# Moving transposes from TensorE to the DMA engines in a fused windowed-attention and SwiGLU kernel, with paced loads

## The chip, the cores and the metric

The kernel runs on one core of one Trainium2 chip. The metric is the time of one execution on the device in microseconds (us); lower is better. Each run lists the clock that was granted to TensorE. Executions of one kernel mostly agree within 0.3 to 1%. A single-core execution counts as slow when it is over 1.5% above the fastest of the same kernel; only fast ones are compared here, by the ratios; the medians below are of all runs.

Names: TensorE is PE in the profile (PEld is its weight load), VectorE is DVE, ScalarE is ACT, GpSimd is POOL and SyncE is SP. GpSimd and SyncE also issue the DMA transfers; each engine has one queue of instructions.

## The reference, cut to what matters

```python
# attention: 4 sequences, 8 heads, 768 tokens, 64 wide; 4 sink tokens, window of 128
scores = q @ k.T / sqrt(64)
keep = (key < 4) | ((0 <= query - key) & (query - key < 128))
a = softmax(where(keep, scores, -1e9)) @ v
# then, with x = a as (3072 tokens, 512):
xn = x / rms(x) * rms_g
out = (silu(xn @ w_gate) * (xn @ w_val)) @ w_out      # 512 -> 1536 -> 512
```

The window of 128 means that the keys of one block of 128 tokens are read by the queries of that block and of the next one.

## The kernel before

The 3072 tokens are 24 blocks of 128, six to a sequence. The FFN takes four blocks (a group) at a time. TensorE does FFN matmuls of one group while the attention units of later blocks are woven in between, one block per `step`.

q and k come in with tokens on the partitions, and the score matmuls need them transposed, in the tile `qkT` of a sequence. Blocks 0 to 12 and 18 are transposed by TensorE (eight 128x128 transposes, then copies out of PSUM), the others by DMA transposes from SyncE's queue:

```python
def load_block(src, name, g):
    ...
    tl = ld.tile([P, H, D], BF16, name=name)     # 18 buffers each for q and k
    nc.gpsimd.dma_start(out=tl, in_=...)
...
    load_wo(0)
    last_load = load_wo(1)
with tc.issue_after(last_load):                  # all other loads, as early as GpSimd can
    for g in range(2 * GB, NB):
        load_q(g); load_k(g); load_v(g)          # (three lines in the kernel)

def by_dma(g):
    return g >= DMA_T_FROM and g % NT > 0        # 12 and up, never a sequence's first block

def unit_t(g):
    b, t = divmod(g, NT)
    if by_dma(g):
        for i, src in enumerate((QS.pop(g), KS_.pop(g))):
            nc.sync.dma_start_transpose(
                out=QKT[b][:, i, :, t * P:(t + 1) * P], in_=src.rearrange(...))
        return
    ... # TensorE transposes and a ScalarE copy
```

Three consumers of `qkT` matter. The first is the score unit. Note the width of `rhs`: up to 256 queries, this block's and the next one's.

```python
def unit_s(g):
    b, t = divmod(g, NT)
    nq = 2 if t + 1 < NT else 1
    w = nq * P
    ...
            nc.tensor.matmul(out=..., lhsT=QKT[b][pr, 1, hp, t * P:(t + 1) * P],
                             rhs=QKT[b][pr, 0, hp, t * P:t * P + w], ...)
```

The second is a pair of tiny VectorE copies that gather the four sink keys of a sequence out of its first block:

```python
def unit_sink(b):
    ks = sink.tile([P, HP * KSW], BF16, name="ksk")
    nc.vector.memset(ks, 0.0)
    ...
    for hi in range(2):
        pr = slice(hi * D, (hi + 1) * D)
        nc.vector.tensor_copy(out=ksv[pr, :, hi * NS:(hi + 1) * NS],
                              in_=QKT[b][pr, 1, :, 0:NS])
```

The third is the sink scores, which come later. The normalized x is transposed the same two ways: by TensorE for blocks 0 to 7, by DMA from block 8 (`DMA_X_FROM`).

The order of instructions is fixed by hand only on TensorE and SyncE (`MANUAL`) in the main part. VectorE, ScalarE and GpSimd get their order from the scheduler that builds the program.

The softmax here doesn't subtract the row's maximum and nothing guards it: scores larger than these inputs give would overflow.

## Time and profile before

| | before |
|---|---|
| time, median of 3 | 254.26 us |
| span of the profiled run | 252.6 us |
| TensorE busy | 95% |
| VectorE busy | 72% |
| q and k transposes on TensorE / by DMA (blocks) | 14 / 10 |

From the page of the kernel before: the span, the busy time of each engine, and some rows of the table in 40 slices of 6.3 us (each digit is tenths busy; PEclk is the granted clock in tenths).

```profile
span 252.6 us, 4804 instructions
PE 238.8 (95%) x1733; PEld 127.4 (50%) x1760; DVE 181.1 (72%) x474; ACT 139.6 (55%) x312; POOL 98.1 (39%) x129
...
PE   5988979989999999999999999999999999999994
...
DVE  5666869889779999539989459988359991287700
...
PEclk9999999999999999999999999999999999999999
DMA  9999999999999999650120550321321013200022
```

TensorE is full from about slice 10 (60 us) on, and its clock is never cut. The DMA engines are full for the first 16 slices (to about 101 us; the prediction below says 110), because all loads are issued as early as possible.

The waits of TensorE in the kernel before (what waited, for whom, us in total, times, longest):

```profile
PE pqk L251 <- DMA qs<-in_q_dram: 1.3, 2, 0.7
...
PE pqk L251 <- DMA ks<-in_k_dram: 1.0, 2, 0.6
```

These 2.3 us are TensorE's transposes of blocks 5 and 8 waiting for their loads.

How long a DMA transpose takes from issue to landing depends on what else is on the engines. Two answers of the issue table of the kernel before, one for 70 to 80 us and one for 120 to 140 us (destination, source, queue, operation, count, median us to landing):

```profile
qkT<-qs SPq DMA_TRANSPOSE x1, 8.3
qkT<-ks SPq DMA_TRANSPOSE x1, 8.2
```

```profile
qkT<-qs SPq DMA_TRANSPOSE x1, 2.4
qkT<-ks SPq DMA_TRANSPOSE x1, 2.4
```

Amid the loads it is 8 us, on quiet engines 2.4 us.

### The profile page before, as it was taken

How to read it: one execution, taken by the hardware profiler on the slowest of the kernel's cores; microseconds unless marked ns; L12 is line 12 of the kernel's file. 1: busy time of each engine (PE TensorE's matmuls, PEld its weight loads, DVE VectorE, ACT ScalarE, POOL GpSimd, SP SyncE). 2: the span in 40 equal slices, each digit the busy share in tenths (PEclk: the TensorE clock that was granted, in tenths of full speed). 3: DMA queues.
4: the chain of work that ended last, by engine and by line, in shares of the span. 5: the costliest groups of instructions: out<-in, count | busy, mean ns of one | idle time of the engine just before them, and what ended most of it. 6: DMA issues, size and time to landing. Idle time of an engine off the chain costs nothing.

```text
span 252.6 us, 4804 instructions
## 1 busy us (share of the span) xinstructions
PE 238.8 (95%) x1733; PEld 127.4 (50%) x1760; DVE 181.1 (72%) x474; ACT 139.6 (55%) x312; POOL 98.1 (39%) x129
## 2 busy tenths in 40 slices
PE   5988979989999999999999999999999999999994
PEld 1446858655555454454454454454454544444441
DVE  5666869889779999539989459988359991287700
ACT  2757858879886465556473546466545441323211
POOL 8996779289985763134041004044201000000000
PEclk9999999999999999999999999999999999999999
DMA  9999999999999999650120550321321013200022
GB/s 130 152 174 189 189 156 188 182 155 150 194 186 161 155 131 155 128 168 13 21 56 10 145 145 3 64 58 19 113 84 23 0 21 98 91 0 0 0 86 83
DMA packets 105850, 25.74 MB, mean 102 GB/s; under 512 B 95074, under 2 KB 102754, under 8 KB 105827
## 3 DMA queue, kind: packets, MB, share of 16 engines
q0 software_dynamic: 80704, 13.90, 76.5%
q1 hardware_dynamic: 24082, 11.28, 18.6%
q10 hardware_dynamic: 1040, 0.26, 0.5%
q8 instruction: 14, 0.23, 0.4%
q14 instruction: 10, 0.07, 0.1%
HBM read 28.31 MB, written 6.29 MB: 137 GB/s over the span
## 4 chain that ended last, share of the span: by engine, by line
PE 67%; DMA 12%; DVE 8%; POOL 7%; ACT 2%; issue 2%; POOLq 0%; ACTq 0%; DVEq 0%
PE po L622 23%; PE pvl L581 18%; PE pg L581 18%; DMA wv<-in_moe_w_val_dram 7%; DMA ks<-in_k_dram 5%; PE pT L413 3%; DVE p L599 2%; POOL v L124 2%; POOL qs L111 2%; DVE hT L607 2%; PE pv L456 1%; PE pv L452 1%; PE pv L444 1%; POOL ks L111 1%; ACT et L422 1%
## 5 line engine op out<-in xcount | busy, mean ns | idle before, releaser
L581 PE MATMUL pg<-xnt,wg 128*128 128x512 bf16 (+1 forms) x317 | 73.5, 352 | 1.1 <-ACT xnt L567 0.5
L581 PE MATMUL pvl<-xnt,wv 128*128 128x512 bf16 (+1 forms) x322 | 73.4, 353 | 0.4
L622 PE MATMUL po<-wo,hT 128*128 128x512 bf16 x279 | 64.9, 379 | 0.5 <-issue 0.2
L594 ACT ACTIVATE th<-pg 128x512 bf16<-128x512 f32 x72 | 42.9, 596 | 39.1 <-PE pg L581 39.0
L599 DVE SCALAR_TENSOR_TENSOR p<-th,pg 128x512 bf16<-128x512 bf16 x72 | 48.9, 679 | 20.1 <-ACT th L594 19.5
L607 DVE TENSOR_TENSOR hT<-p,pvl 128x512 bf16<-128x512 bf16 x72 | 49.2, 684 | 3.7 <-PE pg L581 0.5
L581 PEld LDWEIGHTS <-wv 128*128 128x128 bf16 x328 | 30.5, 98 | 27.2 <-issue 1.1
L581 PEld LDWEIGHTS <-wg 128*128 128x128 bf16 x328 | 30.4, 98 | 26.9 <-issue 1.2
L422 ACT ACTIVATE et<-pT 128x512 bf16<-128x512 f32 x76 | 39.8, 602 | 4.8 <-PE pT L413 4.6
L390 POOL TENSOR_SCALAR_AFFINE_SELECT et<-et 128x512 bf16<-128x512 bf16 x20 | 13.1, 660 | 73.9 <-ACT et L422 73.9
L622 PEld LDWEIGHTS <-hT 128*128 128x128 bf16 x288 | 26.7, 98 | 29.7 <-issue 0.8
L494 ACT ACTIVATE sq<-x 128x256 bf16<-128x256 bf16 x48 | 20.0, 417 | 26.5 <-DVE x L484 26.1
L629 ACT ACTIVATE osb<-po 128x512 f32<-128x512 f32 x24 | 14.4, 602 | 25.9 <-PE po L622 20.8
L111 POOL DMA_DIRECT2D qs<-in_q_dram x23 | 20.7, 900 | 7.9 <-DMA wo<-in_moe_w_out_dram 2.2
L124 POOL DMA_DIRECT2D v<-in_v_dram x24 | 21.7, 903 | 4.4 <-DMA qs<-in_q_dram 2.6
L111 POOL DMA_DIRECT2D ks<-in_k_dram x23 | 20.6, 895 | 6.4 <-DMA wo<-in_moe_w_out_dram 3.2
L484 DVE TENSOR_TENSOR x<-pv,rden 128x256 bf16<-128x256 f32 x48 | 20.2, 421 | 0.8
L541 DVE SCALAR_TENSOR_TENSOR xr<-x,y,gb 128x512 bf16<-128x512 bf16 (+1 forms) x25 | 19.8, 795 | 0.7
L479 DVE RECIPROCAL rden<-pv 128x4 f32<-128x4 f32 x48 | 8.4, 175 | 16.1 <-PE pv L456 16.0
L388 DVE TENSOR_TENSOR et<-et,masks 128x1024 bf16<-128x1024 bf16 (+1 forms) x22 | 13.9, 638 | 3.5 <-ACT et L422 3.5
L456 PE MATMUL pv<-v,et 128*128 128x65 bf16 x168 | 15.3, 193 | 0.0
L452 PE MATMUL pv<-v,et 128*128 128x65 bf16 x136 | 12.7, 193 | 0.0
(75 smaller groups left out, 213.1 us busy)
## 6 DMA issues: line engine op xcount, KB each, us to landing
out_dram<-osb SPq DMA_DIRECT2D x24, 256.0 KB, 2.2
v<-in_v_dram POOLq DMA_DIRECT2D x24, 128.0 KB, 7.9
qs<-in_q_dram POOLq DMA_DIRECT2D x23, 128.0 KB, 8.2
ks<-in_k_dram POOLq DMA_DIRECT2D x23, 128.0 KB, 7.7
wg<-in_moe_w_gate_dram POOLq DMA_DIRECT2D x6, 256.0 KB, 7.6
wv<-in_moe_w_val_dram POOLq DMA_DIRECT2D x6, 256.0 KB, 8.2
wo<-in_moe_w_out_dram POOLq DMA_DIRECT2D x2, 768.0 KB, 10.6
osb<-in_k_dram ACTq DMA_DIRECT2D x1, 256.0 KB, 4.8
```

Of the source, the lines that this page charges most:

```text
L111: nc.gpsimd.dma_start(out=tl, in_=src[b, :, t * P:(t + 1) * P, :].rearrange("h t d -> t h d"),)
L124: nc.gpsimd.dma_start(out=V16[b][:, t, :, 0:D], in_=v[b, :, t * P:(t + 1) * P, :].rearrange("h t d -> t h d"),)
L422: nc.scalar.activation(out=et[:, hi].rearrange("p j n c -> p (j n c)"), in_=banks[u][hi], func=ACT.Exp, scale=inv_sqrt_d,)
L456: nc.tensor.matmul(out=dest, lhsT=E[(g, h, 0)], rhs=V16[b][:, t, h, :], start=(t == 0), stop=True, skip_group_check=True,)
L484: nc.vector.tensor_tensor(out=X16[g][:, heads_of(g, u), :], in0=pvv[:, :, 0:D], in1=RDEN.pop((g, u)).unsqueeze(2).to_broadcast((P, 4, D)), ...
L494: nc.scalar.activation(out=sq, in_=xh, func=ACT.Square, scale=MS_SCALE, accum_out=MS[g][:, u:u + 1],)
L541: nc.vector.scalar_tensor_tensor(out=XR[g][-1], in0=x16[:, c], scalar=y[:, 4:5], in1=gb[:, c], op0=ALU.mult, op1=ALU.mult,)
L581: nc.tensor.matmul(out=ps[:, i * n:(i + 1) * n], lhsT=w_sb[:, kt, ft * P:(ft + 1) * P], rhs=XNT[G][:, kt, cols], start=(kt == 0), stop=(kt ...
L594: nc.scalar.activation(out=st["th"], in_=st["pg"], func=ACT.Tanh, scale=0.5)
L599: nc.vector.scalar_tensor_tensor(out=p1, in0=st["th"], scalar=1.0, in1=st["pg"], op0=ALU.add, op1=ALU.mult,)
L607: nc.vector.tensor_tensor(out=HT[key][:, i:i + n, cols], in0=p1.rearrange("p (n c) -> p n c", n=n), in1=pvl.rearrange("p (n c) -> p n c", ...
L622: nc.tensor.matmul(out=st["po"], lhsT=HT[(G, ft // 2)][:, ft % 2, tb * P:(tb + 1) * P], rhs=wo[:, ft, :], start=(ft == 0), stop=(ft == FTN ...
```

## The change

The intent is to relieve TensorE, the fullest engine: transpose q and k from block 5 on, and x from block 4 on, with the DMA engines. The loads are thinned so that the transposes meet less traffic: q and k get four buffers each, so a load waits until the transposes of an earlier block have read their buffer. GpSimd's order is fixed by hand.

```diff
-    DMA_T_FROM = 12
-    DMA_X_FROM = 8
+    DMA_T_FROM = 5
+    DMA_X_FROM = 4
+    LD = 4
+    AHEAD = 6
-    MANUAL = {mybir.EngineType.PE, mybir.EngineType.SP}
+    MANUAL = {mybir.EngineType.PE, mybir.EngineType.SP, mybir.EngineType.Pool}
-    ld = ctx.enter_context(tc.tile_pool(name="ld", bufs=3 * NT))
+    ld = ctx.enter_context(tc.tile_pool(name="ld", bufs=LD))
...
-    with tc.issue_after(last_load):
-        for g in range(2 * GB, NB):
-            load_q(g)
-            load_k(g)
-            load_v(g)
...
     def by_dma(g):
-        return g >= DMA_T_FROM and g % NT > 0
+        return g >= DMA_T_FROM
...  (in step)
-        if g + 2 < NB and not by_dma(g + 2):
-            slots[2 if t != 5 else 1].append(lambda: unit_t(g + 2))
-        if g + 3 < NB and by_dma(g + 3):
+        if g + 3 < NB:
             slots[2].append(lambda: unit_t(g + 3))
+        if g + AHEAD < NB:
+            slots[2].append(lambda: unit_load(g + AHEAD))
...
-        slots = [[lambda: unit_t1(5, 0)], [lambda: unit_t1(5, 1)], [lambda: unit_s(4)], ...
+        slots = [[lambda: unit_t(5)], [lambda: unit_load(8)], [lambda: unit_s(4)], ...
```

The new `by_dma` has lost `g % NT > 0`. The first block of sequences 1, 2 and 3 (blocks 6, 12, 18) is now transposed by DMA too.

More of the change, by code (lines that the diff above doesn't have):

```diff
@@ L238 @@
         load_wo(0)
-        last_load = load_wo(1)
-    with tc.issue_after(last_load):
-        for g in range(2 * GB, NB):
-            load_q(g)
-            load_k(g)
-            load_v(g)
+        load_wo(1)
     QKT, KSK, VSK, ESK, E, X16, MS, XR, XNT = {}, {}, {}, {}, {}, {}, {}, {}, {}
@@ L267, in unit_t1, with unit_load @@
         )
+    def unit_load(g):
+        load_q(g)
+        load_k(g)
+        load_v(g)
     def by_dma(g):
-        return g >= DMA_T_FROM and g % NT > 0
+        return g >= DMA_T_FROM
     def unit_t(g):
@@ L734 @@
         ], first=True)
-        slots = [[lambda: unit_t1(5, 0)], [lambda: unit_t1(5, 1)], [lambda: unit_s(4)], [lambda: unit_sink_scores(0, 4)], [lambda: unit_t(6)], []]
+        slots = [[lambda: unit_t(5)], [lambda: unit_load(8)], [lambda: unit_s(4)], [lambda: unit_sink_scores(0, 4), lambda: unit_load(9)], [lambda: unit_t(6)], [lambda: unit_t(7), lambda: unit_load(10)]]
         for g in range(5, NB + 3):
```

## The prediction

> **What bounds it now.** From about 60 us on, TensorE: the windows view has it 99% busy from 60 to 240 us, and the matmuls started, counted by columns at the pipelined rate that the chain shows (four of 512 columns in 0.86 us), fill 9.5 to 10.1 of each 10 us. At 30–40 and 50–60 us the same count gives 8.0. There the chain of waits runs through loads (the value weights, then k of block 8: 12.5 us from issue to landing), and TensorE's transposes wait for q and k loads, 2.3 us in all (waits view). The page shows the DMA engines at 9 tenths until 110 us: all loads are issued as early as possible. VectorE is close behind: 92% busy at 50–60, 97% at 80–100 us.
>
> **What the change removes.** TensorE transposed q and k for 14 blocks and will for 5: 72 fewer; x for 8 blocks and will for 4: 16 fewer. Four start within 0.22 us in the timeline, so 88 cost 4.9 us. The 2.3 us of waits for loads (blocks 5 and 8) leave TensorE too, and 0.6 us of waits for xr. ScalarE loses about 11 us of copies, worth nothing: it is 55% busy.
>
> **What it adds.** 18 DMA transposes of q/k and 4 of x, each 1.2 us of issue on SyncE's queue, which has room. Landing takes 2.4 us on quiet engines, but 7 to 8 us between 72 and 95 us, where loads saturate them. The Trainium skill ("DMA: Bandwidth & Descriptors", Queues, rings and completion order) says that each DMA engine takes turns between rows by packet, which fits this.
>
> **Critical path.** The weak spot is block 5. Its q and k land at 35.1 and 35.9 us; two issues end near 37.6; landing at 5 to 7.5 us puts the pair at 42.5 to 45. Its scores ran at 42.2 us before; without the transposes and waits ahead of them TensorE would be there at about 39.5. So I expect a new stall of 3 to 5 us there, which eats the early gain. Blocks 6 and 7 should be just in time; block 8 (k landed at 51.6 us, behind wo) may stall up to 1 us. After that the pacing thins the loads, transposes land in 2.4 to 4 us, over a step ahead of use, and the remaining removals (blocks 9–12 and 18, x 4–7) are real. Buffers of four hold up no early load: the transposes that free them precede those issues in the old trace. GpSimd's fixed order should cost nothing. VectorE at 50–100 us may hold back 1 us.
>
> Sum: -4.9 -2.3 -0.6 +3.5 (stalls) +1 (VectorE) = -3.3; stalls may be shorter, so I say -4.
>
> **Predicted: 250.2 us, range 247.0 to 253.3.** Faster by over 2%: 0.36; within 2%: 0.61; slower by over 2%: 0.03.
>
> **What would show it.** 40 q/k transposes left on TensorE of 112, 16 of x of 32; TensorE waiting for a DMA of qkT before block 5's scores, 3 to 5 us in all; DMA digits below 9 from about 50 us but above zero until about 190 us; DMA transposes' median landing under 4 us; ScalarE 11 us less busy.
>
> **What would make it wrong.** Transposes landing in 3 us at 37 us: no stall, near 247. Landing over 8 us, or stalls repeated at blocks 6 to 8: near 254. VectorE the real limit at 50–100 us: no gain there. Masks on GpSimd queued behind loads that wait for buffers: attention late from block 13 on.

## The result, and the profile after

| | before | changed |
|---|---|---|
| time, median of 4 | 254.23 us | 282.31 us |
| ratio, 95% interval | | 1.1105 [1.1058, 1.1153] |
| TensorE busy | 95% | 85% |
| mean granted clock of the profiled run | 1.0 | 0.957 |

A ratio is the mean time of one kernel's fast runs over the mean of the other's fast runs of the same rounds, so it is not quite the ratio of the medians. The changed kernel is correct and 11% slower; the predicted range ended at 253.3 us.

The same lines of the page, for the changed kernel (slices of 7.0 us):

```profile
span 280.1 us, 4727 instructions
PE 239.2 (85%) x1672; PEld 124.1 (44%) x1672; DVE 179.9 (64%) x473; ACT 129.8 (46%) x299; POOL 97.9 (35%) x129
...
PE   6889700099878999999984999999999999999994
...
DVE  5666400569986399973956865798935998067710
...
PEclk9999975579999999999998999999999999999999
DMA  9999999999399999959992999420332100310012
```

The span is longer by 27.5 us and TensorE's busy time is about what it was: the time went into idleness. There is a hole: TensorE shows zeros from 35 to 56 us and VectorE from 35 to 49 us, and in it the clock falls to 5 tenths. Two groups of instructions of the changed kernel's page name it (busy us, mean ns, then idle time of the engine just before them and what ended most of it):

```profile
L298 DVE COPY ksk<-qkT 64x16 bf16<-64x16 bf16 x8 | 1.4, 174 | 31.2 <-DMA qkT<-ks 31.1
L564 PE MATMUL pxt<-ident,xr 128*128 128x128 bf16 x16 | 2.0, 243 | 22.0 <-DVE xr L542 21.9
```

Eight sink-key copies, 1.4 us of work together, have 31.2 us of idle VectorE in front of them. TensorE in turn waits 21.9 us for an xr of VectorE. In the kernel before, the same copies had 0.3 us of idle time before them:

```profile
L297 DVE COPY ksk<-qkT 64x16 bf16<-64x16 bf16 x8 | 1.9, 234 | 0.3 <-ACT qkT L286 0.2
```

VectorE in order of time, 30 to 53 us of the changed kernel (start, duration, instruction, in brackets the idle time before it and who ended it):

```profile
29.81 0.75 DVE L542 SCALAR_TENSOR_TENSOR xr<-x,y,gb 128x512 bf16<-128x512 bf16 x1
...
30.81 0.68 DVE L600 SCALAR_TENSOR_TENSOR p<-th,pg 128x512 bf16<-128x512 bf16 x1
51.99 0.35 DVE L298 COPY ksk<-qkT 64x16 bf16<-64x16 bf16 x2 [20.50 <-DMA qkT<-ks]
52.37 0.16 DVE L504 SCALAR_TENSOR_TENSOR m<-ms 128x1 f32<-128x1 f32 x1
```

Nothing runs on VectorE between 31.5 and 52.0 us. TensorE in the same stretch:

```profile
32.46 1.04 PE L582 MATMUL pvl<-xnt,wv 128*128 128x256 bf16 x8
54.74 0.61 PE L564 MATMUL pxt<-ident,xr 128*128 128x128 bf16 x4 [21.25 <-DVE xr L542]
56.02 1.87 PE L582 MATMUL pg<-xnt,wg 128*128 128x256 bf16 x8 [0.67 <-ACT xnt L568]
```

The queues of the two built programs, which can be listed without running them, show why. VectorE's rows in the kernel before, around the copies of sequence 1:

```
81 L541 TensorScalarPtr xr_720<-x16_677,y_714,gb_97 128x512      (xr of block 3)
82 L264 TensorCopy qkT_284<-pqk_785 128x4x128
...
92 L607 TensorTensor hT_590<-p1_903,pvl_894 128x2x256
93 L297 TensorCopy ksk_1164<-qkT_883 64x4x4 x2                    (sink keys of sequence 1)
```

and in the changed kernel:

```
73 L600 TensorScalarPtr p1_684<-th_657,pg_648 128x512
74 L298 TensorCopy ksk_1073<-qkT_803 64x4x4 x2                    (sink keys of sequence 1)
75 L504 TensorScalarPtr m_632<-ms_601 128x1
...
82 L542 TensorScalarPtr xr_640<-x16_597,y_634,gb_97 128x512      (xr of block 3)
```

In the program text the copies come much later, in step 7. With block 6 no longer transposed by TensorE, whose order is fixed by hand, the scheduler was free to put its reader on VectorE ahead of block 3's xr. On the chip the transpose of block 6's k landed near 52 us, and everything behind the copies waited. The Trainium skill ("TensorE: Matmul & The Clock Gate", specification table) calls VectorE's queue "strict FIFO", which means that it works its instructions off in order; the 20.5 us of idle time agree.

The landings, from the issue table of the changed kernel for 38 to 40.9 us (block 6's q and k):

```profile
qkT<-qs SPq DMA_TRANSPOSE x1, 10.4
qkT<-ks SPq DMA_TRANSPOSE x1, 12.4
```

Over the whole changed kernel the medians are 5.2 us (q) and 4.6 us (k), against 2.4 us before.

The first theory, called Q below, is therefore: the place of the sink-key copies in VectorE's queue costs the time. Rivals: T, the DMA transposes land too late for TensorE itself, and VectorE only shows it; P, the paced loads and GpSimd's order do it. Later names: S, saturated engines make the landings late and the deadline is a block earlier than predicted; P2, the four-deep buffers hold up loads; H, x transposes stand ahead of q and k transposes in SyncE's queue.

### The profile page after: what moved, and what is told of

It reads as the page before. It is cut to its first block, busy times and chain, and to the rows that moved or that the text cites. A ratio compares the mean times of both kernels' runs of the same rounds, so it can differ in the third digit from the quotient of the medians.

```text
span 280.1 us, 4727 instructions
## 1 busy us (share of the span) xinstructions
PE 239.2 (85%) x1672; PEld 124.1 (44%) x1672; DVE 179.9 (64%) x473; ACT 129.8 (46%) x299; POOL 97.9 (35%) x129
## 4 chain that ended last, share of the span: by engine, by line
PE 59%; DMA 19%; DVE 13%; POOL 4%; issue 2%; ACT 1%; SPq 1%; POOLq 0%; DVEq 0%; ACTq 0%
PE po L623 20%; PE pvl L582 17%; PE pg L582 16%; DMA qkT<-ks 8%; DVE hT L608 3%; DMA wv<-in_moe_w_val_dram 3%; DVE p L600 3%; DMA ks<-in_k_dram 3%; DMA qs<-in_q_dram 3%; PE pT L414 2%; DMA qkT<-qs 2%; DVE xr L542 2%; DVE et L389 2%; PE pv L457 1%; PE pv L453 1%
## 5 line engine op out<-in xcount | busy, mean ns | idle before, releaser
L582 PE MATMUL pg<-xnt,wg 128*128 128x512 bf16 (+1 forms) x328 | 75.5, 359 | 2.5 <-ACT xnt L568 1.1
L582 PE MATMUL pvl<-xnt,wv 128*128 128x512 bf16 (+1 forms) x328 | 75.0, 357 | 0.7 <-DVE p L600 0.6
L623 PE MATMUL po<-wo,hT 128*128 128x512 bf16 x288 | 66.1, 379 | 0.8 <-DVE hT L608 0.8
L582 PEld LDWEIGHTS <-wg 128*128 128x128 bf16 x328 | 31.1, 99 | 30.5 <-issue 4.4
L112 POOL DMA_DIRECT2D ks<-in_k_dram x23 | 20.4, 888 | 12.2 <-DMA qkT<-ks 10.7
L298 DVE COPY ksk<-qkT 64x16 bf16<-64x16 bf16 x8 | 1.4, 174 | 31.2 <-DMA qkT<-ks 31.1
L564 PE MATMUL pxt<-ident,xr 128*128 128x128 bf16 x16 | 2.0, 243 | 22.0 <-DVE xr L542 21.9
L414 PE MATMUL pT<-qkT 64*128 64x256 bf16 (+1 forms) x168 | 13.3, 268 | 7.6 <-DVE p L600 4.2
```

The costliest lines, as they stand in the source:

```text
L112: nc.gpsimd.dma_start(out=tl, in_=src[b, :, t * P:(t + 1) * P, :].rearrange("h t d -> t h d"),)
L414: nc.tensor.matmul(out=banks[u][hi][:, j * w:(j + 1) * w], lhsT=QKT[b][pr, 1, hp, t * P:(t + 1) * P], rhs=QKT[b][pr, 0, hp, t * P:t * P + ...
L582: nc.tensor.matmul(out=ps[:, i * n:(i + 1) * n], lhsT=w_sb[:, kt, ft * P:(ft + 1) * P], rhs=XNT[G][:, kt, cols], start=(kt == 0), stop=(kt ...
L623: nc.tensor.matmul(out=st["po"], lhsT=HT[(G, ft // 2)][:, ft % 2, tb * P:(tb + 1) * P], rhs=wo[:, ft, :], start=(ft == 0), stop=(ft == FTN ...
```

## The experiments

| run | what | median us | ratio to before |
|---|---|---|---|
| (changed) | the whole change | 282.31 | 1.1105 |
| e3_ksk_order_only | changed, copies moved back | 268.75 | 1.0528 |
| e6_block6_alone | before, only block 6 by DMA | 273.09 | 1.0696 |
| e13_block6_order | the same, copies moved back | 262.10 | 1.0244 |
| e4_pacing_only | before, with the new loads | 254.82 | 0.9984 |
| e1_first_blocks_on_pe | changed, 6, 12, 18 on TensorE | 265.88 | 1.0434 |
| e7_order_unpaced | e3 with the old loads | 273.10 | 1.0724 |
| e11_wo_later | e3 with wo behind block 8 | 274.09 | 1.0688 |
| e8_from10_x4 | e3, q and k by DMA from block 10 | 259.04 | 1.0154 |
| e9_from10_x8 | e8, x by DMA from block 8 | 254.45 | 1.0001 |
| e10_from10_no_order | e8 without moving the copies | 269.48 | 1.0539 |
| e14_transposes_ahead_of_x | e8, other order on SyncE | 261.93 | 1.0275 |
| e12_from10_8_before_wo | e9, block 8 loaded before wo | 254.67 | 0.9953 |

All gave correct results. The kernel before had medians of 254.68 to 255.53 us beside them; use the ratios between batches. The medians of e9 and e11 hold one slow run each, those of e10 and e12 two; the ratios leave these out.

### e3_ksk_order_only: only the place of the copies

```diff
-            nc.vector.tensor_copy(
-                out=ksv[pr, :, hi * NS:(hi + 1) * NS],
-                in_=QKT[b][pr, 1, :, 0:NS],
-            )
+            with tc.issue_after(LAST_XR[0]) if b > 0 else ExitStack():
+                nc.vector.tensor_copy(...)          # same copy
...  (in unit_xr)
+            LAST_XR[0] = nc.vector.scalar_tensor_tensor(...).ins
```

A listing of the built queues showed VectorE's to differ from the changed kernel's in the place of the copies of sequences 1, 2 and 3 and in nothing else.

> The changed kernel with one thing different: the small VectorE copies that gather the sink keys of sequences 1, 2 and 3 (they read the transposed k of blocks 6, 12, 18) stand later in VectorE's queue, behind the latest xr written before them in the program. Every transfer, buffer and other order is as in the changed kernel. Theory Q (queue order: these copies stand at the head of VectorE's in-order queue long before their DMA transposes land, and hold back everything behind them): the 20.5, 5.3 and 5.4 us idle times of VectorE before these copies go, TensorE's 21.2 us wait for xr goes, and the time falls from 282.3 to 257 us (253 to 262); what stays over 254 is TensorE waiting some 5 to 10 us for DMA transposes of blocks 5, 6 and 8, which landed after 7.6 to 12.4 us. Rival T (late transposes are the cause themselves; VectorE only shows them): TensorE now waits for the same landings at its scores, some 15 to 20 us, and the time stays at 272 us or more. Rival P (the paced loads and GpSimd's order): no change from 282.

Measured: 268.75 us. VectorE no longer waits before the copies, and TensorE's 21 us wait for xr is gone. That is 13.6 us by the medians (about 14.7 by the ratios), from moving six tiny copies. But the time lies between what Q and T expected, because a second wait surfaced. The waits of TensorE in this run:

```profile
PE pT L415 <- DMA qkT<-qs: 14.6, 4, 6.9
```

pT are the scores. In order of time:

```profile
43.92 1.03 PE L415 MATMUL pT<-qkT 64*128 64x256 bf16 x8 [6.86 <-DMA qkT<-qs]
51.01 0.40 PE L415 MATMUL pT<-qkT 64*128 64x128 bf16 x8
56.62 0.61 PE L415 MATMUL pT<-qkT 64*128 64x256 bf16 x8 [0.91 <-DMA qkT<-qs]
65.00 1.04 PE L415 MATMUL pT<-qkT 64*128 64x256 bf16 x8 [4.36 <-DMA qkT<-qs]
...
79.54 0.72 PE L415 MATMUL pT<-qkT 64*128 64x256 bf16 x8 [2.46 <-DMA qkT<-qs]
```

The second line is 128 wide, so it is block 5, the last of its sequence. The line before it is block 4's scores, and they wait for the q of block 5. That is the `rhs` of 256 queries in `unit_s`. In the kernel before, block 4's scores ran at 37.15 us without a wait:

```profile
37.15 0.61 PE L413 MATMUL pT<-qkT 64*128 64x256 bf16 x8
```

The deadline that I had taken, block 5's own scores at 42.18 us, was one block too late. Blocks 6, 7 and 9 wait for the q of 7, 8 and 10 in the same way.

### e6_block6_alone and e13_block6_order: one block, then one block and the order

```diff
 (e6, on the kernel before)
-        return g >= DMA_T_FROM and g % NT > 0
+        return g == 6 or g >= DMA_T_FROM and g % NT > 0
```

> The kernel before with one thing different: block 6 (the first of sequence 1) has its q and k transposed by the DMA engines instead of TensorE, at the same place in the program; all loads are early as before. Theory Q: the scheduler again puts the sink-key copies of sequence 1 ahead of block 3's xr in VectorE's queue (the queue of the built kernel shows it), so VectorE sits idle from about 32 us until the k transpose of block 6 lands, some 7 us after its issue near 39 us; TensorE loses 12 to 15 us, time 266 us (262 to 271), from two transfers out of a kernel's thousands of instructions. Rival T: block 6's scores ran at 47.3 us and the transpose lands at about 46 to 47: no loss, 254 (252 to 256). Rival P: 254.

Measured: 273.09 us, more than Q expected, and far from the 254 of T and P. Two DMA transposes cost 18 us. In the groups of this run the copies show it:

```profile
L297 DVE COPY ksk<-qkT 64x16 bf16<-64x16 bf16 x8 | 1.6, 196 | 17.8 <-DMA qkT<-ks 17.5 <-ACT qkT L286 0.2
```

The k transpose was issued at 39.5 and the copies could start at 50.55 us, a landing of 11.1 us, not the 7 that I used. e13 adds to this the same order fix as in e3.

> The kernel before with only block 6 transposed by the DMA engines (273.1 us with the sink-key copies where the scheduler put them), and those copies moved behind the latest xr before them. Same two DMA transposes, same loads. Theory Q: nearly all of the 18 us goes; TensorE waits for block 6's transpose itself only from block 6's scores on (block 5 is the last of its sequence and does not read block 6), 47.3 us before, and that transpose landed at 50.3: 3 us at most, 256.5 us (254.5 to 258.5). If the copies' place were not the cause, 265 or more.

Measured: 262.10 us, ratio 1.0244 [1.0173, 1.0315], which leaves open whether it is over 2% slower than the kernel before; it is clearly faster than e6 (1.0696). The order is worth 11 of the 18 us; my figure of nearly all was too high. (A few neighbouring VectorE and ScalarE instructions swap places too in the built queues of e13; in e3 none do.) What remains is block 6's own scores waiting for its k, and what that wait does to the clock. TensorE in order of time, then the windows (us, then busy us and count of PE, PEld, DVE, ACT, POOL, then PEclk, DMA share, GB/s):

```profile
47.01 1.04 PE L583 MATMUL pg<-xnt,wg 128*128 128x256 bf16 x8
52.62 1.03 PE L414 MATMUL pT<-qkT 64*128 64x256 bf16 x8 [4.57 <-DMA qkT<-ks]
53.58 1.89 PE L583 MATMUL pvl<-xnt,wv 128*128 128x256 bf16 x8
```

```profile
48.00:50.00 2.00, 0.05 (x1) 0.00 (x0) 1.58 (x4) 0.60 (x1) 0.81 (x1) 1.00 1.23 195
...
52.00:54.00 2.00, 1.38 (x11) 0.73 (x12) 0.00 (x0) 0.74 (x2) 0.38 (x1) 0.50 2.35 158
54.00:56.00 2.00, 2.00 (x17) 1.57 (x16) 1.02 (x4) 1.71 (x5) 1.81 (x3) 0.50 2.50 154
56.00:58.00 2.00, 2.00 (x11) 0.90 (x9) 2.00 (x7) 0.07 (x1) 1.85 (x3) 0.50 2.71 150
58.00:60.00 2.00, 2.00 (x26) 1.44 (x25) 1.80 (x5) 1.54 (x2) 1.86 (x3) 0.90 2.88 149
```

Eight matmuls of 256 columns take 1.04 us before the wait and 1.89 us after it: after the wait the clock stays halved for about 6 us, of which half, an estimated 3 us, is lost. The Trainium skill ("TensorE: Matmul & The Clock Gate", Why this matters for your kernels) says to leave no idle gaps of more than about 3 us for this reason, and the trace agrees: a wait of 4.6 us costs more than 4.6 us. The limit is not sharp in these runs: a wait of 2.5 us in e3 was followed by half clock too (80 to 82 us), one of 2.7 us in e8 was not.

### e4_pacing_only: the new loads without the new transposes

```diff
 (on the changed kernel)
-    DMA_T_FROM = 5
-    DMA_X_FROM = 4
+    DMA_T_FROM = 12
+    DMA_X_FROM = 8
-        return g >= DMA_T_FROM
+        return g >= DMA_T_FROM and g % NT > 0
...  transposes back in their old slots; loads 8, 9 and 10 in the slots beside them
```

> The changed kernel with the transposes of before (DMA transposes from block 12, without first blocks, x from block 8) but the changed loads: four-deep q and k buffers, loads from block 8 on paced six blocks ahead, GpSimd's order by hand. Theory Q: the sink-key copies stand where they stood before, nothing waits, 254 us (251 to 257). Rival P: a large part of the 28 us is here, 265 us or more. Rival T: 254.

Measured: 254.82 us, ratio 0.9984 [0.9952, 1.0017]. Four-deep buffers, paced loads and GpSimd's fixed order cost nothing by themselves. P falls.

### e1_first_blocks_on_pe: the lost condition put back

```diff
     def by_dma(g):
-        return g >= DMA_T_FROM
+        return g >= DMA_T_FROM and g % NT > 0
```

> The changed kernel, but the first block of each later sequence (6, 12, 18) is transposed on TensorE; all other transposes from block 5 on, and x from block 4, stay on the DMA engines. Theory Q: the sink-key copies then wait for nothing late, all three VectorE idle times go; what remains is TensorE waiting for block 5 (about 5 us) and perhaps block 7 or 8: 254 us (250 to 258). Rival T: blocks 5, 7, 8 are as late as before, TensorE waits 10 us or more in all, 262 or more. Rival P: 275 or more.

Measured: 265.88 us. The waits before the copies are gone, as under Q, but TensorE waits 12.1 us for transposed q (the longest is 7.3 us, at block 4's scores). That is the 262 or more that T gave. Both this run and e3 say that two costs lie one behind the other.

### e7_order_unpaced: are the late landings the pacing's fault?

```diff
 (on e3)
-    LD = 4 buffers, unit_load(g + AHEAD) in step, Pool in MANUAL
+    18 buffers, all loads behind load_wo(1), GpSimd's order by the scheduler
```

> The earlier run with the sink-key copies moved (268.75 us) and the old loads again: all q, k and v loads as early as GpSimd can issue them, 18-deep buffers, GpSimd's order left to the scheduler; the transposes on the DMA engines as in the changed kernel. What is left over 254 is TensorE waiting 14.6 us for the transposed q of the next block. Theory S (DMA transposes issued while loads saturate the DMA engines land after 8 to 14 us, and each block's scores need the next block's q, so the deadline is a block earlier than I predicted): loads that are not paced keep the engines saturated, waits of 10 to 15 us stay, 263 to 270 us. Rival P2 (the four buffers: load 8 waited until 44.3 us for block 5's transpose, where it was issued at 38.3 us before): loads 8 to 10 come 5 us earlier, the waits at blocks 7 and 9 go (6.8 us), 260 to 263.

Measured: 273.10 us, a ratio of 1.0724 against 1.0528 with pacing. That is over the 270 at which S ended, so the size was missed, on the side away from P2. TensorE waits 15.1 us for transposed q, and the DMA transposes' median landing is 7.2 us. P2 falls: load 8 is indeed held until 44.3 us in e3, where it was issued at 38.3 before, but without pacing it gets worse. The pacing did what it was meant to do, after block 8.

### e11_wo_later: what makes the landings late?

```diff
 (on e3)
-        load_wo(0)
-        load_wo(1)
...
-        slots = [..., [lambda: unit_load(8)], ...
+        slots = [..., [lambda: unit_load(8), lambda: load_wo(0), lambda: load_wo(1)], ...
```

> The changed kernel with the sink-key copies moved (268.75 us), and the two loads of wo (768 KB each in the transfer list) issued behind the loads of block 8 instead of ahead of them, so that they are not on the DMA engines while blocks 5 to 7 are transposed. Theory S (transposes land late because loads hold the DMA engines): the landings of blocks 5 to 7 fall from 7.6 to 15 us to 5 to 9 us, TensorE's first wait (6.9 us at block 4's scores) to 4 to 5 us, time 263 to 267. Rival (transposes issued back to back hold up each other): landings stay at 8 to 15 us, 268 to 270.

Measured: 274.09 us, a miss in the time. The landings of blocks 6 and 7 did what S expected; those of block 5, 7.5 and 7.6 us, were hardly shorter than in e3 (8.1 and 8.5 us). (The profiled run of e11 just counts as slow, 274.89 us; its mean clock, 0.963, is that of the fast runs.) The issue table of e3 for 35.6 to 41 us and of this run for 36.9 to 42.2 us (in both, blocks 5 and 6):

```profile
qkT<-qs SPq DMA_TRANSPOSE x2, 9.6
qkT<-ks SPq DMA_TRANSPOSE x2, 10.7
```

```profile
qkT<-qs SPq DMA_TRANSPOSE x2, 7.0
qkT<-ks SPq DMA_TRANSPOSE x2, 6.5
```

Block 7's q fell from 15.3 to 4.6 us. The transposes were issued as close together as before, so back-to-back issue is not what made these late. e6 and e13 say the same: block 6's two transposes are the only ones in that stage there, and they landed after 8.6 to 12.2 us. What e11 takes away is wo's loads. How the engines were shared can be read from the DMA queues of the changed kernel at 45 to 50 us (q0 carries the loads, here mostly wo; q1 the transposes; packets, MB, share):

```profile
q0 software_dynamic: 781, 0.78, 92.2%
q1 hardware_dynamic: 776, 0.19, 29.4%
```

The two queues advance packet for packet, as the prediction had it from the skill, but a packet of wo is about 1000 bytes and one of a transpose about 250, so the transposes get a fifth of the bytes. The loads seem to suffer in turn: where the transposes start among the small q, k and v loads, the rate falls to 59 GB/s (changed kernel, 39 to 40 us) and 14 GB/s (e11, 40 to 41 us), while the kernel before stays at 153 or more from 38 to 43 us. No run here isolates the cause of that fall.

But block 4's scores still waited 6.6 us, since block 5's q was loaded 1.2 us later here, and the loads of block 9 now came late behind wo: TensorE waited 8.8 us at 73.9 us. The wait had moved.

### e8_from10_x4 and e9_from10_x8: transposes by DMA only from block 10

```diff
 (e8, on e3)
-    DMA_T_FROM = 5
+    DMA_T_FROM = 10
...  TensorE's transposes at their old places, two blocks ahead
 (e9, on e8)
-    DMA_X_FROM = 4
+    DMA_X_FROM = 8
```

> The changed kernel with both causes taken away: the sink-key copies moved back in VectorE's queue, and DMA transposes of q and k only from block 10 on (blocks 5 to 9 on TensorE at their old places); paced loads and x from block 4 by DMA stay. Theory S with Q: by block 10 (about 57 us) there is at most a small wait; TensorE has 4 x 8 + 16 = 48 transposes fewer than the kernel before, 2.6 us: 252 us (250 to 254). If the waits for transposed q return (over 3 us in all), 255 or more, and block 10 is still too early. Rival P2 or P: 258 or more.

Measured: 259.04 us. The early waits are gone, one of 2.7 us is left. The time is outside the range of S with Q and where P2 or P would have it, but e9, which has the same loads and buffers, rules these two out.

> As the run with DMA transposes from block 10, but x by DMA only from block 8 as before. TensorE has 16 transposes more, 0.9 us, and may wait again for xr of blocks 4 to 7 (0.6 us before): 1 to 1.5 us over the run beside it. If x from block 4 was itself harmful (its transposes delay those of q and k in SyncE's queue), this one is the faster of the two.

Measured: 254.45 us, ratio 1.0001 [0.9981, 1.0020]. I had expected it to be slower than e8, and it is 4.6 us faster by the medians, 3.9 by the ratios: x by DMA from block 4 is harmful. In the two traces the starts of the scores of blocks 4 to 8 agree within 0.6 us, then differ by 3.1 us at block 9 (67.8 and 64.7 us) and by about that to the end. SyncE's queue, e8 first, then e9:

```profile
53.65 7.41 SPq L552 DMA_TRANSPOSE xnt<-xr  x2
61.10 1.27 SPq L279 DMA_TRANSPOSE qkT<-qs  x1
```

```profile
56.76 1.46 SPq L279 DMA_TRANSPOSE qkT<-qs  x1
58.27 1.26 SPq L279 DMA_TRANSPOSE qkT<-ks  x1
```

In e8 two x transposes, which wait for VectorE's xr, stand ahead of block 10's q, and it is issued at 61.1 instead of 56.8 us.

### e10_from10_no_order: the copies again, away from the busy stage

```diff
 (on e8)
-            with tc.issue_after(LAST_XR[0]) if b > 0 else ExitStack():
-                nc.vector.tensor_copy(...)
+            nc.vector.tensor_copy(...)
```

> As the run with DMA transposes from block 10 and x from block 4, but with the sink-key copies where the scheduler puts them. Sequence 1's stand where they stood before (block 6 is on TensorE again); those of sequences 2 and 3 stand early and wait for the DMA transposes of blocks 12 and 18. Theory Q: VectorE sits idle for about 5 us before each of the two, TensorE's wait is somewhat shorter, 6 to 9 us in all over the run with the copies moved: 258 to 261. Rival (the order matters only where the DMA engines are saturated): within 1 us of the run with the copies moved.

Measured: 269.48 us with two slow runs in it; by the ratios of the fast runs it is 9.8 us over e8. VectorE sat idle 12.3 us before the copies of sequences 2 and 3, more than expected. (The profiled run was a slow one; the four fast runs lie between 266.66 and 269.85 us.) The first of the two waits, 7.1 us to 83.6 us, still falls where the DMA digits are at 9. The second, 5.2 us to 138.0 us, falls where they are at 7 and 6, so the order costs time outside the saturated stage too.

### e14_transposes_ahead_of_x: SyncE's order

```diff
 (on e8)
-        if g + 3 < NB and by_dma(g + 3):
-            slots[2].append(lambda: unit_t(g + 3))
+        if g + 4 < NB and by_dma(g + 4):
+            slots[3].insert(0, lambda: unit_t(g + 4))
```

> The run with DMA transposes from block 10, x by DMA from block 4 and the sink-key copies moved (259.0 us, where TensorE waited 2.7 us for block 10's q at block 9's scores and stayed 3.1 us behind its neighbour with x from block 8 from there on), with one thing different: each block's q and k transposes are put into SyncE's queue one slot earlier, ahead of the x transpose of block 5 and so on. Theory H (head of line in SyncE's queue: block 10's transposes were issued at 61.1 us instead of 56.8 because two x transposes ahead of them waited for VectorE): they are issued at about 57 to 58 us, the wait at block 9's scores shrinks to under 1 us, 255.5 us (253.5 to 256.5). Rival (x by DMA costs elsewhere, at the start of the second group or on the DMA engines): 258 or more.

Measured: 261.93 us, slower than e8. H was right about its own step: block 10's q was issued at 57.1 us and the wait at block 9's scores is gone. But the rival was right about the time. TensorE now has one long wait, at the first gate matmul of the second group:

```profile
79.25 1.86 PE L584 MATMUL pg<-xnt,wg 128*128 128x512 bf16 x4 [6.10 <-DMA out_dram<-osb]
```

The transfer named there is the one that ended last by the record. The one that the matmul needs is the x transpose of block 7, issued at 70.0 us with a landing of 9.0 us, which ends at 79.0. By TensorE and a copy, x goes the same way in about 1 us (0.40 and 0.59 us in the trace of before). Both orders tried on SyncE leave one of the two transposes late in this stage.

### e12_from10_8_before_wo: a try at beating both

```diff
 (on e9)
-        load_wo(0)
-        load_wo(1)
...
+        [lambda: unit_t1(5, 1), lambda: unit_load(8), lambda: load_wo(0), lambda: load_wo(1)]
```

> A try at a kernel that beats both: DMA transposes of q and k from block 10, x from block 8, sink-key copies moved, paced loads (254.45 us), and block 8's loads issued ahead of wo's, which GpSimd's hand-fixed order allows. TensorE's wait for block 8's q and k near 51 us (0.8 us here, 1.3 us in the kernel before) goes: 253.5 us (252.5 to 254.5). If wo then lands after the first use near 56 us, 255 or more.

Measured: 254.67 us, of which two runs are slow (the fast ones have a median of 253.9 us); the ratio of the fast runs is 0.9953 [0.9892, 1.0014]. The wait for block 8's load is gone, as expected, but a gain is not shown. No version here clearly beats the kernel before.

## Why the prediction was wrong

The change was predicted as 250.2 us and took 282.3. Taken away one after the other, the parts of the loss are: the order of the copies on VectorE (1.1105 to 1.0528), q and k of blocks 5 to 9 by DMA (to 1.0154), and x of blocks 4 to 7 by DMA (to 1.0001). The shares depend on the order of removal, since the waits hide each other: taking away VectorE's 31 us of waiting gave back only about 14 us, because 14.6 us of waiting on TensorE lay beneath.

Point by point:

- **"GpSimd's fixed order should cost nothing" and "Buffers of four hold up no early load".** The first holds (e4). The second was wrong as a statement: load 8 waited for block 5's DMA transpose, 43.6 us instead of 38.3. It was not the cause of the loss (e4, e7).
- **The critical path: "TensorE would be there at about 39.5. So I expect a new stall of 3 to 5 us there".** This is the step that failed, in three ways.
  - It followed `qkT` only to TensorE. A second reader, on an engine whose order the scheduler chooses, was missed altogether. That reader moved 19 rows up in VectorE's queue and held it for 20.5 us. Shown by e3 (nothing else differs), by e6 and by e13.
  - The deadline was wrong by a block. `unit_s` reads the next block's q, so block 5 was due at 37.15, not 42.18 us. Shown by e3 and e1: 6.9 and 7.3 us at block 4's scores. For the same reason block 8, which was allowed 1 us, came 4.4 us late (e3).
  - "Landing at 5 to 7.5 us" was too short. Blocks 5 to 7 took 7.6 to 13.9 us in the changed kernel, while q, k, v and wo loads were on the engines; e11 took wo away and the landings of blocks 6 and 7 fell.
- **"After that ... transposes land in 2.4 to 4 us".** The medians are 5.2 and 4.6 us. Paced loads are thinner, but they now go on past 110 us, where the engines used to be quiet.
- **"0.6 us of waits for xr" saved by x transposes.** Mis-signed: e8 against e9 shows 3.9 us lost by the ratios, and e14 shows that the loss moves rather than goes.
- **The clock.** I did not count it. Each idle time of 3.7 us or more on TensorE in these traces brought a stretch at half clock (in the changed kernel from the hole until about 59 us); of the five between 2.4 and 3.2 us three did.
- **The gain, "88 cost 4.9 us".** The count was right: 40 q and k transposes and 16 of x are left on TensorE. The worth was too high. e9 has 32 fewer than the kernel before, 1.8 us by the same measure, and its ratio is 1.0001; between block 8's and block 22's scores its trace is 0.8 us shorter. Where the other 1 us goes is argued only: between 152 and 173 us the chains of waits of both kernels run through VectorE and ScalarE, so a faster TensorE waits there.
- **"ScalarE 11 us less busy ... worth nothing".** 9.8 us less, and it bought nothing.

## What to carry to other kernels

When a producer moves to another engine or to DMA, list every reader of its tile, on every engine, and look at the built queues: a scheduler may put a tiny reader ahead of work that the whole kernel waits for, and an in-order queue then turns one late transfer into a stall of everything. Take a deadline from the earliest read of any part of the tile, and the landing time from a transfer of the same kind in the same stage, not from a quiet one. Relieving the fullest engine in a stage where the DMA engines are fuller moves the work to the worse place.

## What the Trainium skill lacked or had wrong

- "Advanced Engine Details and Errata" (X-Bar Transpose (TRN2)) says "TRN2 transpose DMAs are as fast as regular DMAs". On quiet engines the runs come near that (2.4 us to landing for a transpose of 128 KB, against 2.1 to 2.2 us for the output stores of 256 KB), but no page gives the landing of a transpose beside loads of small pieces: mostly 7 to 15 us here, three to six times as long, nor that such loads slow down too (59 and 14 GB/s in the stretches above).
- No page gives the issue time of a 128x512 bf16 transpose from SBUF to SBUF on this chip (there are cycle counts for other sizes on other generations): 1.2 us on SyncE's queue, and up to 4.7 us when the engines are full (e3).
- "TensorE: Matmul & The Clock Gate" (Part 4: PE-mode transpose) puts a 128x128 transpose at about 275 ns in a kernel. Here one lasted 0.22 us, and four in a row started within 0.22 us, so the cost to a full TensorE was 55 ns each.
- The same page has the strict order of VectorE's queue and the halved clock after idle gaps, and both were seen. It counts the cost of half clock too, so nothing is missing there; the runs add one figure, about 6 us at half clock after a wait of 4.6 us.
